# Reading a key/value cache in tiles of four heads instead of two, with half as many buffers

## The chip, the cores and the metric

The kernel runs on one core of a Trainium2 chip; the other cores are idle. The metric is the device time of one execution in microseconds (us). A profile is one execution with the trace on; its span runs from the first to the last instruction and is about 1.7 us shorter than the time of the same execution.

## The reference, cut to what matters

One decoding step for 8 sequences: layer norm, attention of one query per head over a cache of 4096 keys, 32 heads of 128, and in parallel a small MLP. Everything is bfloat16. The two caches together hold 537 MB of the 552 MB that the kernel reads, each byte once, and that is what the time is about.

```python
B, Sq, D = 8, 1, 640;  Hq, Hkv, Sk, Dh = 32, 32, 4096, 128
xn = _layernorm(x)
q = (xn @ wq).reshape(B, Sq, Hq, Dh).transpose(0, 2, 1, 3)
scores = einsum("bhqd,bhkd->bhqk", q, k_cache) * Dh ** -0.5      # k_cache: (8, 32, 4096, 128)
o = einsum("bhqk,bhkd->bhqd", softmax(scores), v_cache)          # v_cache: the same shape
out = x + o.transpose(0, 2, 1, 3).reshape(B, Sq, Hq * Dh) @ wo + mlp(layernorm(xn))
```

## The kernel before

A tile is two adjacent heads of one sequence: 2 MB of keys, or of values, contiguous in memory. It is spread over the 128 partitions so that each reads one run of 16 KB (64 keys of 256 B). Four key buffers and four value buffers of 16 KB per partition rotate.

```python
HT = 2                    # heads of a tile
NJ = SK * HT // P         # 64 keys per partition
T = NG * B                # 128 tiles
GT = 4                    # tiles of a softmax group
NK, NV, NS = 4, 4, 4      # key buffers, value buffers
KV_sb = sb("KV_sb", [P, NK + NV, NJ * P], BF)
...
def tile_src(cache, t):
    return cache[t % B, span(t // B, HT)].rearrange("h k d -> (h k) d").rearrange("(p j) d -> p j d", p=P)
def kpieces(t):
    return [(0, 64)]                                   # one transfer per tile
def vpieces(t):                                        # the last value tile in four transfers
    return [(0, 16), (16, 32), (32, 48), (48, 64)] if t == T - 1 else [(0, 64)]
```

All large loads are issued from the SyncE queue, in order. SyncE waits before each until the buffer is free: a key buffer when VectorE and TensorE have read it, a value buffer when TensorE has.

Per tile, a quarter of the scores is made on TensorE (transposes, ScalarE copies them out of PSUM, short matmuls) and three quarters on VectorE (multiply by the broadcast query, fold once, reduce). A softmax follows per group of tiles. Then TensorE multiplies probabilities with values (`PV_ps`), ScalarE copies the result out, and a few small matmuls gather it (`OT`). After a group of heads, the result is multiplied with rows of `wo` (loaded per group) and added up in PSUM.

```python
add("dve", dp,  mult, ...)        # Y  <- K * q          128 x 6144
add("dve", ..., fold, ...)        # Y2 <- halves added   128 x 3072
add("dve", ..., reduce, ...)      # S  <- sum            128 x 48
...
add("pe",  p0 + 0.15 * q, pe_pv)  # PV <- P^T V          16 matmuls of 512 columns per tile
add("act", p0 + 0.5, evacuate)    # E  <- PV
add("pe",  p0 + 0.8, pe_ex)       # OT <- gather E
```

A small scheduler sorts all operations by a position (the second argument of `add`) on their engine's in-order queue and places the semaphore waits; the steady part is then emitted as a loop.

## Time and profile before

| | before |
|---|---|
| time, median | 1305.2 us (4 runs, 1304.7 to 1305.5) |
| span of the profile | 1303.5 us |
| DMA busy | over 99% |
| rate in the steady part | 427.7 GB/s |
| VectorE, TensorE, ScalarE busy | 85%, 54%, 40% |

From the page of the profile, kernel before: span, busy times by engine, then, for 40 slices of the span, the busy tenths of the DMA engines and what they moved; the packets; the chain of waits by engine.

```profile
span 1303.5 us, 20261 instructions
PE 704.9 (54%) x7741; PEld 401.3 (31%) x7741; DVE 1109.6 (85%) x554; ACT 516.7 (40%) x1264; POOL 0.2 (0%) x4
...
DMA  9999999999999999999999999999999999999997
GB/s 375 423 428 425 427 427 428 429 426 429 425 430 427 428 429 426 429 426 429 427 428 428 427 428 427 428 426 428 427 428 427 428 427 428 427 429 429 425 428 322
DMA packets 45440, 552.03 MB, mean 424 GB/s; under 512 B 4505, under 2 KB 10993, under 8 KB 12786
...
DMA 79%; DVE 11%; PE 9%; issue 1%; ACT 0%; SPq 0%
```

Every slice but the last has the 16 DMA engines at 9 tenths or more, and the rate is flat. The chain of waits is mostly a transfer. So the kernel is bound by DMA, from 2 us to the end, and only three things can shorten it: a higher rate, a DMA queue that fills earlier, or a shorter tail.

Table of windows, kernel before (window and length in us; busy us and number of instructions for TensorE, its weight loads, VectorE, ScalarE, GpSimd; granted TensorE clock; DMA share; GB/s):

```profile
400.00:600.00 200.00, 108.62 (x1157) 60.97 (x1157) 172.96 (x81) 79.84 (x195) 0.00 (x0) 0.53 1.01 427
1290.00:1295.00 5.00, 3.72 (x40) 1.14 (x40) 0.00 (x0) 1.11 (x2) 0.00 (x0) 0.50 0.98 394
1295.00:1300.00 5.00, 3.04 (x74) 1.86 (x71) 0.17 (x1) 0.87 (x2) 0.00 (x0) 0.50 0.20 79
```

The middle is at the steady rate. In the last two windows some engines have run out of work: they do not finish together.

VectorE spends 3.34 + 1.75 + 3.35 = 8.45 us on a tile, in 9.9 us that its key and value tiles take to arrive. It is the next limit, but not the present one.

DMA issues, kernel before (count, KB, median us from issue to landing):

```profile
KV_sb<-in_A_k_cache_dram SPq DMA_DIRECT2D x128, 2048.0 KB, 33.9
KV_sb<-in_A_v_cache_dram SPq DMA_DIRECT2D x127, 2048.0 KB, 31.0
```

A transfer that takes 4.9 us at the steady rate lands 31 to 34 us after it was issued: the work of five or six others stands in the queue ahead of it.

The tail, from the timeline of the kernel before (start us, duration us, engine, line, operation, count):

```profile
1298.38 0.63 PE L609 MATMUL PV_ps<-KV_sb,P_sb 128*2 128x128 bf16 x16 [0.57 <-DMA KV_sb<-in_A_v_cache_dram]
...
1299.88 1.23 PE L644 MATMUL TR_ps<-wo_sb,oTn_sb 128*8 128x320 bf16 x4 [0.26 <-DVE oTn_sb L636]
```

After the last piece of values has landed, 16 narrow matmuls run, and then four for the output.

The trace also has one record per DMA packet, with its size and duration. 10th percentile of the durations, in ns, kernel before:

```
bytes     1280   3456   4096   7168   16384
ns          55    135    159    272     611
```

These lie on a line: 0.0368 ns per byte and 7 to 8 ns per packet.

### The profile page before, as it was taken

To read this page: it belongs to the slowest core of one execution; us is meant where nothing else is said; L and a number is where in the kernel's file an instruction comes from. 1 tells how busy PE (TensorE), PEld (TensorE's weight loads), DVE (VectorE), ACT (ScalarE), POOL (GpSimd) and SP (SyncE) were. 2 spreads that over 40 slices of the span, in tenths; PEclk is the share of its full clock that TensorE was granted. 3 is DMA by queue.
4 is the path that set the end of the run, shared out by engine and by line. 5 is a ranking of instruction groups with operands and counts; after the bars stand their busy time and mean duration, and the time that the engine had idled before them with its cause. 6 is when DMAs were issued, how large, how long until landed. Compare 5 with 4: busy or idle time off the path is not lost.

```text
span 1303.5 us, 20261 instructions
## 1 busy us (share of the span) xinstructions
PE 704.9 (54%) x7741; PEld 401.3 (31%) x7741; DVE 1109.6 (85%) x554; ACT 516.7 (40%) x1264; POOL 0.2 (0%) x4
## 2 busy tenths in 40 slices
PE   2665555555555555545555555555465555555555
PEld 2543223233223223323322232332232333223222
DVE  7989889888898888898888898888988888988881
ACT  2443344434334433433434444343344334434332
POOL 0000000000000000000000000000000000000000
PEclk9999985555555555555555555555556555555555
DMA  9999999999999999999999999999999999999997
GB/s 375 423 428 425 427 427 428 429 426 429 425 430 427 428 429 426 429 426 429 427 428 428 427 428 427 428 426 428 427 428 427 428 427 428 427 429 429 425 428 322
DMA packets 45440, 552.03 MB, mean 424 GB/s; under 512 B 4505, under 2 KB 10993, under 8 KB 12786
## 3 DMA queue, kind: packets, MB, share of 16 engines
q1 hardware_dynamic: 45392, 551.81, 99.9%
q8 instruction: 10, 0.16, 0.1%
q10 hardware_dynamic: 34, 0.02, 0.0%
q14 instruction: 4, 0.03, 0.0%
HBM read 551.80 MB, written 0.01 MB: 423 GB/s over the span
## 4 chain that ended last, share of the span: by engine, by line
DMA 79%; DVE 11%; PE 9%; issue 1%; ACT 0%; SPq 0%
DMA KV_sb<-in_A_k_cache_dram 77%; DVE Y_sb L541 9%; PE TR_ps L509 5%; PE C_ps L586 2%; PE PV_ps L612 1%; DVE S_sb L548 1%; DMA KV_sb<-in_A_v_cache_dram 1%; DMA KV_sb<-in_A_wq_dram 1%; DVE Y_sb L545 1%; ACT P_sb L575 0%; SPq L367 0%; PE TR_ps L720 0%; DVE rinv_sb L591 0%; PE TR_ps L644 0%; PE TR_ps L707 0%
## 5 line engine op out<-in xcount | busy, mean ns | idle before, releaser
L512 ACT ACTIVATE KT_sb<-TR_ps 128x1024 bf16<-128x1024 bf16 x256 | 261.3, 1023 | 637.0 <-PE TR_ps L509 636.6
L509 PE MATMUL TR_ps<-ident_bf,KV_sb 128*128 128x128 bf16 x2048 | 263.6, 311 | 416.5 <-DMA KV_sb<-in_A_k_cache_dram 416.5
L548 DVE TENSOR_REDUCE S_sb<-Y_sb 128x48 f32<-128x3072 bf16 x128 | 429.2, 3353 | 4.4
L541 DVE TENSOR_TENSOR Y_sb<-KV_sb,qbc_sb 128x6144 bf16<-128x6144 bf16 x128 | 427.6, 3340 | 4.4 <-ACT qbc_sb L482 4.4
L509 PEld LDWEIGHTS TR_ps<-ident_bf,KV_sb 128*128 128x128 bf16 x2048 | 197.5, 141 | 551.8 <-DMA KV_sb<-in_A_k_cache_dram 497.6
L612 PE MATMUL PV_ps<-KV_sb,P_sb 128*8 128x512 bf16 x2032 | 279.7, 585 | 39.1 <-DMA KV_sb<-in_A_v_cache_dram 39.0
L545 DVE TENSOR_TENSOR Y_sb<-Y_sb 128x3072 bf16<-128x3072 bf16 x128 | 224.4, 1753 | 2.3
L519 PE MATMUL S_ps<-qk_sb,KT_sb 128*128 128x2 bf16 x2048 | 90.4, 167 | 74.4 <-ACT KT_sb L512 74.4
L519 PEld LDWEIGHTS S_ps<-qk_sb,KT_sb 128*128 128x128 bf16 x2048 | 71.7, 104 | 128.6 <-ACT KT_sb L512 84.5
L591 DVE RECIPROCAL rinv_sb<-C_ps 128x8 f32<-128x8 f32 x32 | 6.6, 207 | 115.5 <-PE C_ps L586 115.5
L575 ACT ACTIVATE P_sb<-S_sb,NB_sb 64x64 bf16<-64x64 f32 x256 | 88.4, 345 | 4.2
L620 ACT ACTIVATE E_sb<-PV_ps 128x512 bf16<-128x512 f32 x128 | 75.6, 591 | 27.3 <-PE PV_ps L612 24.3
L612 PEld LDWEIGHTS PV_ps<-KV_sb,P_sb 128*8 128x8 bf16 x2032 | 39.6, 83 | 92.0 <-issue 45.6
L529 ACT ACTIVATE S_sb<-S_ps 64x16 f32<-64x16 f32 x256 | 45.5, 178 | 6.2 <-PE S_ps L519 4.7
L575 ACT ACTIVATION_READ_ACCUMULATOR P_sb<-S_sb,NB_sb 64x1 f32 x256 | 47.3, 185 | 0.0
L636 DVE TENSOR_TENSOR oTn_sb<-C_ps,rinv_sb 128x8 bf16<-128x8 f32 x32 | 5.3, 166 | 46.7 <-PE C_ps L628 36.6
L628 PE MATMUL C_ps<-sel_bf,E_sb 128*128 128x2 bf16 x508 | 33.1, 170 | 13.0 <-ACT E_sb L620 6.1
L569 ACT ACTIVATE NB_sb<-CH_ps 128x4 f32<-128x4 f32 x32 | 5.5, 173 | 76.6 <-PE CH_ps L565 76.6
L628 PEld LDWEIGHTS C_ps<-sel_bf,E_sb 128*128 128x128 bf16 x508 | 23.2, 105 | 28.1 <-ACT E_sb L620 28.1
L586 PEld LDWEIGHTS C_ps<-rs_sb,mask_f 128*128 128x128 f32 x128 | 31.2, 334 | 0.9 <-issue 0.9
L586 PE MATMUL C_ps<-rs_sb,mask_f 128*128 128x4 f32 x128 | 30.8, 346 | 0.0
L565 PE MATMUL CH_ps<-identneg,M_sb 4*64 4x4 f32 x128 | 11.5, 244 | 24.8 <-DVE M_sb L560 24.8
(81 smaller groups left out, 174.0 us busy)
## 6 DMA issues: line engine op xcount, KB each, us to landing
KV_sb<-in_A_k_cache_dram SPq DMA_DIRECT2D x128, 2048.0 KB, 33.9
KV_sb<-in_A_v_cache_dram SPq DMA_DIRECT2D x127, 2048.0 KB, 31.0
wo_sb<-in_A_wo_dram SPq DMA_DIRECT2D x16, 320.0 KB, 30.5
KV_sb<-in_A_wq_dram SPq DMA_DIRECT2D x1, 4480.0 KB, 16.0
KV_sb<-in_B_w_dram SPq DMA_DIRECT2D x1, 2160.0 KB, 20.0
KV_sb<-in_B_w_dram SPq DMA_DIRECT2D x1, 2080.0 KB, 24.8
KV_sb<-in_A_v_cache_dram SPq DMA_DIRECT2D x4, 512.0 KB, 11.8
KV_sb<-in_A_wq_dram SPq DMA_DIRECT2D x1, 640.0 KB, 9.5
```

Of the source, the lines that this page charges most:

```text
L509: r = e.transpose(TR_ps[:, it.box[0], jj * P:(jj + 1) * P], kv[:, n * BK + jj, :], ident_bf[:, :])
L512: add("act", t - 0.55 + 0.2 * n, lambda e: e.activation(KT_sb[:, m % NS, :, :].rearrange("p a b -> p (a b)"), TR_ps[:, it.box[0], :], ACT. ...
L519: r = e.matmul(S_ps[:, c:c + HT], KT_sb[:, m % NS, jj, :], qk_sb[:, :, b], start=True, stop=True)
L529: r = e.activation(S_sb[s, g % SR, i, 0:JP], S_ps[s, 0:JP * HT].rearrange("p (j a) -> p j a", a=HT)[:, :, a], ACT.Copy)
L541: return e.tensor_tensor(y, kv[:, j0:j1, :], qbc_sb[:, g % 2, i, :][:, None, :].to_broadcast([P, nj, P]), ALU.mult)
L545: lambda e, y=y, y2=y2: e.tensor_tensor(y2, y[:, :, 0:P // 2], y[:, :, P // 2:P], ALU.add),
L548: lambda e, y2=y2, j0=j0, j1=j1: e.tensor_reduce(S_sb[:, g % SR, i, j0:j1], y2, AX.X, ALU.add),
L575: r = e.activation(P_sb[s, g % PR, i, :, a, :], S_sb[s, g % SR, i, :].rearrange("p (m c) -> p m c", c=4), ACT.Exp, bias=NB_sb[s, g % 2, i: ...
L586: r = e.matmul(RS_ps[:, a * GT:(a + 1) * GT], mask_f[:, a, :], rs_sb[:, g % PR, :], start=True, stop=True)
L612: r = e.matmul(PV_ps[32 * ct:32 * ct + HT * 4, t % 2, :], P_sb[:, g % PR, i, m, :, :].rearrange("p a c -> p (a c)"), vv[:, 4 * m:4 * m + 4 ...
L620: add("act", p0 + 0.5, lambda e: e.activation(E_sb[:, t % 2, 0:ne], PV_ps[:, t % 2, 0:ne], ACT.Copy), R=[("PV", t % 2)], W=[("E", t % 2)], ...
L628: r = e.matmul(o, E_sb[:, t % 2, c * P:(c + 1) * P], sel_bf[:, c:HT * 4:4], start=(c == 0), stop=(c == 3))
```

## The change

A tile becomes four adjacent heads: 4 MB, and a run of 32 KB per partition. Since buffers are twice as large, there are two for keys and two for values. The intent is fewer and longer DMA packets at the same memory. The rest follows from it: softmax groups of two tiles, TensorE's loop over half a group of heads, work with larger tiles cut in two, the early loads reordered, the MLP's second weights in a buffer of their own, and a reworked end.

```diff
-    HT = 2
+    HT = 4
-    GT = 4
+    GT = 2
+    HB = B // 2
-    NK, NV, NS = 4, 4, 4
+    NK, NV, NS = 2, 2, 4
...
+        w2_sb = sb("w2_sb", [P, FC, D], BF)
-        Y_sb = sb("Y_sb", [P, ND, P], BF)
+        Y_sb = sb("Y_sb", [P, ND // 2, P], BF)
...
-            ld(1.9, wqb_sb, A_wq[:, QP * P:H * P]..., ["wqB"], "wqb", ["ovfree"])
+            ld(-93.0, wqb_sb, A_wq[:, QP * P:H * P]..., ["wqB"], "wqb")
 def vpieces(t):
-    return [(0, 16), (16, 32), (32, 48), (48, 64)] if t == T - 1 else [(0, 64)]
+    return [(0, 64), (64, 96), (96, NJ)] if t == T - 1 else [(0, NJ)]
...
-            pos = (-100.0, -98.0, -94.0, -93.0)[t] if t < NK else t - 3.6
+            pos = (-100.0, -94.0)[t] if t < NK else t - 1.5          # key tiles
-            pos = (1.95, 5.6, 5.65, 6.0)[t] if t < NV else pvpos(t - NV) + 0.95
-            R = (["wqAfree"] if t == 0 else ["wqBfree", "ovfree"]) if t < NV else []
+            pos = t + 0.6                                            # value tiles
+            R = (["wqBfree"], ["wqBfree", "wqAfree", "ovfree"])[t] if t < NV else []
...
-            cuts = [(JP, NJ)]
+            cuts = [(JP, JP + ND // 2), (JP + ND // 2, NJ)]
...
-            sch.emit_rolled("pe", e, sems, 6.43, B)
+            sch.emit_rolled("pe", e, sems, 2.013, HB)
```

The first value buffer still holds query weights at the start (`wqb_sb`); `wqBfree` is given when TensorE has computed the queries from them.

## The prediction

> **What bounds the kernel now.** The page: 16 DMA engines busy 99.9% of 1303.5 us, 552 MB at 424 GB/s; a table of windows: 427 to 428 GB/s from 200 to 1250 us. The chain of waits is 77% key-cache DMA. VectorE (85%), TensorE (54%) and ScalarE (40%) all have slack. The outer ends: the first packet starts 2 us in, and after the last value piece lands (PE goes on at 1298.4 us) 5 us of tail remain. [...]
>
> **What the change gives.** The trace's packet records: typical durations 55 ns (1280 B), 135 (3456), 159 (4096), 272 (7168), 611 (16384). That is a line of 0.0368 ns per byte plus 7 to 8 ns per packet. A 32 KB run as one packet should take about 1215 ns, not 1222. Each engine carries about 2040 of the 16 KB packets; 1020 times 7.3 ns saved is 7.4 us. Half as many transfers also save 127 completion packets of 9 ns per engine, 1.1 us. All of it is on the critical path: together 8.5 us. Nothing else in the steady state moves the time, as bytes are equal.
>
> **Does the DMA queue stay full with two buffers?** A pair of 4 MB tiles takes 19.6 us (twice the 9.8 us of today's pair). VectorE needs per tile 2 x (3.34 + 1.75 + 3.35) = 16.9 us plus about 0.6 for maxima and reciprocals, under 19.6. A key buffer is given back 17.5 us after landing, when two transfers, V(t-1) and K(t+2)'s slot, order the queue: K(t+2) must be issued by 29.4 us after K(t) landed. Slack about 12 us. Values have more. TensorE needs about 10 us per tile. VectorE now waits for the wo weights once in eight tiles; they land about 3 us late for it; the slack covers that.
>
> **Start and end.** Before key tile 2, 18 MB are issued without waiting, drained near 47 us. Value tile 0 overwrites the query weights, so it waits for seven projection rounds of about 1 us (measured: 0.7 us TensorE + 0.2 us ScalarE + hand-overs) after they land: about 56 us, while K2 ends at 56.5. I expect a gap of 0 to 4 us there, 1 to 2 likely. The tail grows: 32 narrow matmuls instead of 16 (0.6 to 1.0 us) and 8 output matmuls instead of 4 (1.2 to 2.4 us): +1.6 us.
>
> Sum: 1305.2 - 8.5 + 1.5 + 1.6, rounded down for the other early work, about **1299 us**, range 1291 to 1307. Chances: faster by over 2% 0.04, within 2% 0.93, slower by over 2% 0.03.
>
> **Right or wrong in the profile.** Right: packets of 32768 B near 1215 to 1225 ns; windows at 429 to 431 GB/s; DMA busy over 99%; busy times of VectorE and TensorE nearly unchanged, ScalarE a little up; SyncE's waits end long before the queue empties. Wrong: 16 KB packets still (no gain, about 1308), windows below 427 GB/s or slices with DMA under 9 tenths (buffers too few), a hole of over 5 us near 57 us.
>
> **What would break it.** [...] the engines drifting apart by whole 1.2 us packets, which lengthens the end; VectorE waiting on TensorE for maxima or reciprocals long enough to eat the 12 us of slack.

1305.2 - 8.5 + 1.5 + 1.6 = 1299.8 us, put at 1299. The 9 ns of a completion packet are in the trace of the kernel before: 4506 packets of 4 bytes, about 16 for each of the 280 loads from SyncE's queue, with a mean of 9.0 ns.

## More of the kernel before

Groups of instructions, kernel before (busy us in all, mean ns of one):

```profile
L548 DVE TENSOR_REDUCE S_sb<-Y_sb 128x48 f32<-128x3072 bf16 x128 | 429.2, 3353 | 4.4
L541 DVE TENSOR_TENSOR Y_sb<-KV_sb,qbc_sb 128x6144 bf16<-128x6144 bf16 x128 | 427.6, 3340 | 4.4 <-ACT qbc_sb L482 4.4
...
L545 DVE TENSOR_TENSOR Y_sb<-Y_sb 128x3072 bf16<-128x3072 bf16 x128 | 224.4, 1753 | 2.3
...
L620 ACT ACTIVATE E_sb<-PV_ps 128x512 bf16<-128x512 f32 x128 | 75.6, 591 | 27.3 <-PE PV_ps L612 24.3
```

## The result, and the profile after

| | before | after |
|---|---|---|
| time, median | 1305.2 us (4 runs) | 1298.78 us (4 runs, 1298.17 to 1301.47) |
| span of the profile | 1303.5 us | 1297.0 us |
| first packet to last value packet | 1296.0 us | 1288.7 us |
| last value packet to end of span | 5.6 us | 6.5 us |

The ratio is 0.9955, with a 95% interval of 0.9938 to 0.9972. Ratios here are the mean time of one kernel's fast runs over that of the other's of the same rounds, so not quite the ratio of the medians. The kernel is faster by 0.5%, which is within 2%.

The same lines of the page, kernel after:

```profile
span 1297.0 us, 19542 instructions
PE 657.6 (51%) x7884; PEld 428.4 (33%) x7884; DVE 1119.4 (86%) x574; ACT 493.1 (38%) x1202; POOL 0.2 (0%) x4
...
DMA  9999999999999999999999999999999999999997
GB/s 383 399 425 433 431 429 434 426 434 432 428 435 425 436 434 428 432 425 436 434 431 431 425 435 435 431 429 431 429 435 431 429 431 429 436 430 426 433 430 302
DMA packets 26738, 552.04 MB, mean 426 GB/s; under 512 B 2313, under 2 KB 8801, under 8 KB 10082
...
DMA 86%; PE 9%; DVE 2%; SPq 2%; issue 1%; ACT 0%; DVEq 0%
```

There are 26,738 packets instead of 45,440, and the steady slices are higher: the 64 + 64 cache tiles now move in packets of 32 KB. But the second slice is lower than it was (399 against 423 GB/s), and so is the last. The clock line of TensorE is not shown; it is at 9 tenths or more in the first slice and at 5 or 6 after it, where the kernel before had 8 or 9 tenths in its first six slices and 5 or 6 after them.

Table of windows, kernel after:

```profile
50.00:60.00 10.00, 8.04 (x175) 7.16 (x173) 4.85 (x2) 4.42 (x10) 0.00 (x0) 0.50 0.91 356
400.00:600.00 200.00, 101.02 (x1182) 65.24 (x1180) 174.94 (x84) 77.39 (x189) 0.00 (x0) 0.54 1.01 431
1280.00:1290.00 10.00, 8.52 (x76) 2.96 (x76) 0.22 (x2) 1.88 (x6) 0.00 (x0) 0.71 0.77 320
1290.00:1295.00 5.00, 3.10 (x45) 1.41 (x42) 0.47 (x2) 0.58 (x2) 0.00 (x0) 0.77 0.00 2
```

In 400 to 600 us the rate is 431 GB/s against 427. The window 50 to 60 us has a hole: 356 GB/s at a DMA share of 0.91.

Groups, kernel after (the same VectorE work and ScalarE copy):

```profile
L544 DVE TENSOR_TENSOR Y_sb<-KV_sb,qbc_sb 128x6144 bf16<-128x6144 bf16 x128 | 429.1, 3352 | 93.9 <-DMA KV_sb<-in_A_k_cache_dram 93.9
L551 DVE TENSOR_REDUCE S_sb<-Y_sb 128x48 f32<-128x3072 bf16 x128 | 429.1, 3353 | 4.4
...
L548 DVE TENSOR_TENSOR Y_sb<-Y_sb 128x3072 bf16<-128x3072 bf16 x128 | 224.9, 1757 | 4.4
...
L638 ACT ACTIVATE E_sb<-PV_ps 128x512 bf16<-128x512 f32 (+1 forms) x65 | 38.5, 592 | 319.8 <-PE PV_ps L619 317.9
```

VectorE does the same 128 rounds in the same time. ScalarE's copy out of PSUM now occurs 65 times instead of 128, because a tile of four heads fills the same 512 columns; this saves it 37 us of busy time. ScalarE has no share in the chain that ended last (ACT 0%), so it saves nothing else.

DMA issues, kernel after:

```profile
KV_sb<-in_A_k_cache_dram SPq DMA_DIRECT2D x64, 4096.0 KB, 26.8
KV_sb<-in_A_v_cache_dram SPq DMA_DIRECT2D x63, 4096.0 KB, 35.2
```

A transfer takes 9.7 us now. A key tile lands 26.8 us after its issue, so about 17 us of work stand ahead of it. Two buffers are enough.

Waits of VectorE, kernel after (total us, times, longest us):

```profile
DVE Y_sb L544 <- DMA KV_sb<-in_A_k_cache_dram: 93.9, 53, 2.3
DVE oTn_sb L661 <- issue: 22.5, 8, 3.1
```

VectorE waits a little for key tiles, which is how a DMA-bound kernel should look, and eight times for the weights of `wo`, never longer than 3.1 us. (The profile names no releaser for the latter, only "issue"; but each of the seven long waits ends 0.04 us after a load of `wo` has landed.)

The hole, from the timeline of the kernel after, SyncE's issues (key tile 2, value tile 0, key tile 3):

```profile
30.97 0.34 SPq L370 DMA_DIRECT2D KV_sb<-in_A_k_cache_dram  x1
56.29 0.34 SPq L370 DMA_DIRECT2D KV_sb<-in_A_v_cache_dram  x1
60.43 0.33 SPq L370 DMA_DIRECT2D KV_sb<-in_A_k_cache_dram  x1
```

And TensorE's query projections, the first and the last of seven rounds, same kernel:

```profile
48.85 0.69 PE L457 MATMUL C_ps<-xnT_sb,KV_sb 128*128 128x8 bf16 x20 [16.87 <-DMA KV_sb<-in_A_wq_dram]
...
55.56 0.70 PE L457 MATMUL C_ps<-xnT_sb,KV_sb 128*128 128x8 bf16 x20 [0.29 <-ACT qT_sb L462]
```

Value tile 0 goes into the buffer of the query weights. They land at 48.8 us, the last round has started at 55.6 us, and the load is issued at 56.3 us, when the DMA engines have just drained key tile 2. By the packet records, 1.1 us of all 16 engines are lost there.

The balance can be read from the bytes moved by a given time (from the packet records):

```
MB moved by      50 us    60 us    200 us   1200 us   1285 us
before           19.51    23.71     83.44    511.17    547.45
after            19.59    23.10     83.31    514.25    550.84
```

From 60 to 1285 us the kernel after gains 4.00 MB, which is 9.3 us at 431 GB/s. It starts that stretch 0.61 MB behind (1.4 us, the hole and the restart after it), and the engines end 0.5 us more apart. That leaves 7.4 us, by which the last value packet comes earlier (1290.5 instead of 1297.9 us). The tail is 0.9 us longer.

### The profile page after: what moved, and what is told of

It reads as the page before. It is cut to its first block, busy times and chain, and to the rows that moved or that the text cites. A ratio compares the mean times of both kernels' runs of the same rounds, so it can differ in the third digit from the quotient of the medians.

```text
span 1297.0 us, 19542 instructions
## 1 busy us (share of the span) xinstructions
PE 657.6 (51%) x7884; PEld 428.4 (33%) x7884; DVE 1119.4 (86%) x574; ACT 493.1 (38%) x1202; POOL 0.2 (0%) x4
## 2 busy tenths in 40 slices
DMA packets 26738, 552.04 MB, mean 426 GB/s; under 512 B 2313, under 2 KB 8801, under 8 KB 10082
## 4 chain that ended last, share of the span: by engine, by line
DMA 86%; PE 9%; DVE 2%; SPq 2%; issue 1%; ACT 0%; DVEq 0%
DMA KV_sb<-in_A_v_cache_dram 84%; PE PV_ps L619 8%; DMA KV_sb<-in_A_wq_dram 2%; SPq L370 2%; DVE Y_sb L544 1%; DVE Y_sb L548 0%; PE C_ps L457 0%; PE TR_ps L512 0%; ACT KT_sb L515 0%; PE TR_ps L669 0%; ACT qT_sb L462 0%; ACT S_sb L532 0%; PE PV_ps L629 0%; PE S_ps L522 0%; DVE out_sb L749 0%
## 5 line engine op out<-in xcount | busy, mean ns | idle before, releaser
L619 PE MATMUL PV_ps<-KV_sb,P_sb 128*16 128x512 bf16 x2040 | 224.6, 619 | 130.4 <-DMA KV_sb<-in_A_v_cache_dram 130.4
L522 PE MATMUL S_ps<-qk_sb,KT_sb 128*128 128x4 bf16 x2048 | 97.9, 170 | 147.4 <-ACT KT_sb L515 145.8
L638 ACT ACTIVATE E_sb<-PV_ps 128x512 bf16<-128x512 f32 (+1 forms) x65 | 38.5, 592 | 319.8 <-PE PV_ps L619 317.9
L522 PEld LDWEIGHTS S_ps<-qk_sb,KT_sb 128*128 128x128 bf16 x2048 | 86.1, 109 | 178.2 <-ACT KT_sb L515 178.2
L619 PEld LDWEIGHTS PV_ps<-KV_sb,P_sb 128*16 128x16 bf16 x2040 | 63.1, 124 | 242.9 <-DMA KV_sb<-in_A_v_cache_dram 136.0
L583 ACT ACTIVATE P_sb<-S_sb,NB_sb 32x128 bf16<-32x128 f32 x256 | 101.9, 398 | 3.8
L644 PE MATMUL C_ps<-sel_bf,E_sb 128*128 128x4 bf16 x256 | 16.9, 172 | 102.6 <-DVE rinv_sb L600 79.3
L532 ACT ACTIVATE S_sb<-S_ps 32x32 f32<-32x32 f32 x256 | 48.2, 188 | 31.5 <-PE S_ps L522 29.2
L583 ACT ACTIVATION_READ_ACCUMULATOR P_sb<-S_sb,NB_sb 32x1 f32 x256 | 47.0, 184 | 0.0
L595 PE MATMUL C_ps<-rs_sb,mask_f 128*128 128x2 f32 x256 | 45.4, 299 | 0.0
L661 DVE TENSOR_TENSOR oTn_sb<-C_ps,rinv_sb 128x8 bf16<-128x8 f32 x32 | 4.7, 147 | 26.8 <-issue 22.5
## 6 DMA issues: line engine op xcount, KB each, us to landing
KV_sb<-in_A_k_cache_dram SPq DMA_DIRECT2D x64, 4096.0 KB, 26.8
KV_sb<-in_A_v_cache_dram SPq DMA_DIRECT2D x1, 2048.0 KB, 12.7
```

Source lines behind the costliest of these rows:

```text
L522: r = e.matmul(S_ps[:, c:c + HT], KT_sb[:, m % NS, jj, :], qk_sb[:, :, b % HB], start=True, stop=True)
L532: r = e.activation(S_sb[s, g % SR, i, 0:JP], S_ps[s, 0:JP * HT].rearrange("p (j a) -> p j a", a=HT)[:, :, a], ACT.Copy)
L583: r = e.activation(P_sb[s, g % PR, i, :, a, :], S_sb[s, g % SR, i, :].rearrange("p (m c) -> p m c", c=4), ACT.Exp, bias=NB_sb[s, g % 2, i: ...
L595: r = e.matmul(RS_ps[:, a * GT:(a + 1) * GT], mask_f[:, a, :], rs_sb[:, g % PR, :], start=True, stop=True)
L619: r = e.matmul(PV_ps[32 * ct:32 * ct + HT * 4, t % 2, :], P_sb[:, g % PR, i, m, :, :].rearrange("p a c -> p (a c)"), vv[:, 4 * m:4 * m + 4 ...
L638: add("act", pos, lambda e: e.activation(E_sb[:, k, 0:n], PV_ps[:, k, 0:n], ACT.Copy), R=[("PV", k)], W=[("E", k)], X=[("PVb", k)])
```

## The experiments

The edited kernels start from the kernel after; where one builds on another edit, it says so. All results were correct. "Tile time" is the time per 4 MB of cache in the steady part: from the packet records, the time between the reading of one amount of cache and the same amount plus 96 tiles of 4 MB, over 96. It includes a sixteenth of a load of `wo`, and repeats to 0.002 us between the three traces of the kernel after. The expectations give the tail (last value packet to end of span) 0.25 us shorter than this document: packet times had first been read 0.25 us late against the instructions.

Theory P: the gain in the steady part is a fixed cost per DMA packet. Rivals: the other parts of the change (S), easier addresses for the memory (A), or the number of transfers (T).

### The kernel after, once more (a0_again)

> The changed kernel once more, as the reference for the others of this call and to see its spread (one of its first four times was 1301.5, the other three 1298.2 to 1298.8). Every theory: 1298 to 1302 us.

Measured: 1299.75 us (1297.81, 1300.93, 1301.30, 1298.57), ratio 0.9960 to before. The spread is in two groups, which comes up again below. Kernel before in these rounds: 1305.39 us.

### Packets of 16 KB in two transfers (e1_two_16k)

```diff
 def kpieces(t):
-    return [(0, NJ)]
+    return [(0, 64), (64, 128)]
 def vpieces(t):
-    return [(0, 64), (64, 96), (96, NJ)] if t == T - 1 else [(0, NJ)]
+    return [(0, 64), (64, 96), (96, NJ)] if t == T - 1 else [(0, 64), (64, 128)]
```

> Changed kernel, but every tile of 4 MB is loaded by two transfers, each with runs of 16 KB: the packets and the number of transfers are those of the kernel before, everything else is the change's. Theory P (the gain is a fixed cost of about 7 ns per packet and 9 ns per completion): packets of 611 to 615 ns, steady rate back to 427.7 GB/s, and 8 to 9 us lost: about 1307 us, over the kernel before, whose start has no hole. Rival S (the gain comes from the other parts, the order of the early loads, the smaller tail, the half quads): time stays at 1299.

Measured: 1310.52 us (1309.16 to 1311.56), 10.8 us over the kernel after. Kernels are compared only within the same rounds. Window of the steady part, this run:

```profile
400.00:600.00 200.00, 102.36 (x1174) 65.12 (x1173) 173.64 (x84) 75.94 (x185) 0.00 (x0) 0.51 1.01 427
```

The rate is that of the kernel before, and the tile time is 9.903 us: before it was 9.903 us too, and after it is 9.828 us. So the whole gain in the steady part hangs on the size of the packets or on the number of transfers, and rival S is out: the other parts of the change are all present here, and the time is worse than before. That it is 3.5 us over the expected 1307 is partly the larger cost per packet and partly this run's tail, of 8.7 us.

### Packets of 16 KB in one transfer (e5_one_16k)

```diff
-        KV_sb = sb("KV_sb", [P, NK + NV, NJ * P], BF)
+        PAD = 32                                  # 64 bytes between the halves of a buffer
+        HJ = NJ // 2
+        HW = HJ * P + PAD
+        KV_sb = sb("KV_sb", [P, NK + NV, 2 * HW], BF)
...
+                return s.rearrange("p (h j) d -> p h (j d)", h=2)   # the source: 128 x 2 x 8192
...
-            cuts = [(JP, JP + ND // 2), (JP + ND // 2, NJ)]
+            cuts = [(JP, HJ), (HJ, HJ + 32), (HJ + 32, NJ)]
```

> Changed kernel, one transfer per 4 MB tile as there, reading the same addresses in the same order per partition, but 64 bytes of padding between the halves of each buffer so that a run written is 16 KB; VectorE takes three cuts of 32 columns instead of two of 48 for that. Theory P: packets of 16 KB at 611 to 615 ns, 7.4 us lost, about 1306 us (1 us less than with two transfers). Rival A (longer runs are easier on the memory, whatever the packet): the addresses read are unchanged, so about 1299. If the queue makes 32 KB packets in spite of the padding, it says nothing.

Measured: 1307.36 us (1305.25 to 1309.58, in two groups), packets of 16 KB, tile time 9.879 us. Window of the steady part, this run:

```profile
400.00:600.00 200.00, 102.34 (x1188) 66.73 (x1185) 177.68 (x115) 76.69 (x188) 0.00 (x0) 0.54 1.01 428
```

The addresses read are those of the kernel after, in the same order per partition, and 0.051 of the 0.075 us per tile are lost all the same. So most of the gain is not in the addresses (rival A): shorter packets alone cost it. The remaining 0.025 us per tile between this run and the last would fit a cost per transfer, but see the run with every second partition.

### Packets of 8 KB (e2_four_8k)

```diff
 def kpieces(t):
-    return [(0, NJ)]
+    return [(0, 32), (32, 64), (64, 96), (96, 128)]
```

and the same for the value tiles but the last.

> Changed kernel, every tile by four transfers with runs of 8 KB. From the time per 4 MB tile in three traces (9.828 us with 32 KB, 9.879 with 16 KB in one transfer, 9.903 with 16 KB in two) come 6.4 ns per packet and 24.5 ns per transfer; with 16 packets per engine and two transfers more that makes 10.055 us per tile, and 127.5 tiles x 0.152 us = 19 us more than the run with two transfers of 16 KB: about 1328 us. Packet records of 309 to 315 ns. If the law is wrong and small runs cost more than their packets (or the memory minds), the time is well above 1332; if only the packet's own 7.3 ns count, 1325.

Measured: 1327.46 us (two runs), ratio 1.0168; tile time 10.055 us. Window of the steady part, this run:

```profile
400.00:600.00 200.00, 102.39 (x1145) 59.62 (x1144) 170.35 (x82) 74.92 (x185) 0.00 (x0) 0.51 1.01 421
```

The time came out as expected, but it does not test the split in the expectation, since packets and transfers grow together here. The tile times are on a straight line in the number of packets per engine, 8, 16 and 32:

```
                       packets per engine and 4 MB      tile time, us       difference per packet
after                         8                             9.828
two transfers of 16 KB       16                             9.903              0.0757 / 8  = 9.5 ns
four transfers of 8 KB       32                            10.055              0.1513 / 16 = 9.5 ns
```

So a packet costs 9.5 ns beside its bytes, where each 8 packets come with a transfer of their own.

### Twice the transfers, packets of 32 KB: halves of the partitions (e3_half_parts)

```diff
-                ld(pos + 0.01 * n, kview(t)[:, j0:j1, :], lambda ...: tile_src(A_k_cache, t)[:, j0:j1, :], ...)
+                for u in range(2):
+                    s = slice(64 * u, 64 * u + 64)
+                    ld(pos + 0.01 * n + 0.005 * u, kview(t)[s, j0:j1, :],
+                       lambda ...: tile_src(A_k_cache, t)[s, j0:j1, :], ...)
```

and the same for values; readers wait for both halves.

> Changed kernel, every tile loaded by two transfers of 64 partitions each, runs of 32 KB: the number of transfers of before, the packets of after. Theory P: only the 9 ns completions come back, 1.1 us: about 1300 us. Rival T (it is the number of transfers that costs, not the packets): about 1306 or more. [...]

Measured: 2602.69 us, ratio 1.9932. Window of the steady part, this run:

```profile
400.00:600.00 200.00, 48.89 (x598) 32.34 (x598) 86.48 (x40) 36.45 (x87) 0.00 (x0) 0.55 1.01 211
```

Neither theory expected this. All engines are busy (DMA share 1.01), yet the rate is half, and a packet of 32 KB takes 2391 to 2564 ns instead of 1213 to 1221 (10th and 90th percentile). The 211 GB/s are close to half of 430.9, the steady rate of the kernel after; why the rate halves, this run does not show.

### Twice the transfers, packets of 32 KB: every second partition (e8_alternate)

```diff
-                    s = slice(64 * u, 64 * u + 64)
+                    s = slice(u, P, 2)
```

(from the kernel with halves)

> The run with half partitions again, but a transfer now takes every second partition instead of one half of the partitions: again 64 partitions and runs of 32 KB per transfer, twice the transfers. Theory H (what halved the rate there was that all 16 engines write into one half of the partitions at once): rate back to 430 GB/s, packets near 1215 to 1225 ns, and the cost of twice the transfers alone, which the runs with 16 KB put at 24 ns each, so 3 us: about 1302 us. Rival N (64 partitions per transfer are slow whatever they are, or two transfers per tile are): 2600 us again.

Measured: 1299.22 us (1298.85 to 1301.55), ratio 0.9951; tile time 9.828 us. Window of the steady part, this run:

```profile
400.00:600.00 200.00, 102.75 (x1186) 67.44 (x1183) 175.07 (x85) 77.03 (x187) 0.00 (x0) 0.54 1.00 430
```

The full rate is back with 64 partitions per transfer and two transfers per tile, so it was which partitions, not how many. By what means they halve the rate, no trace shows. It also decides rival T: twice as many transfers, with the packets unchanged, cost nothing that the tile time shows. The expected 24 ns per transfer fell. The gain is in the packets. What the 0.025 us between one and two transfers of 16 KB is, stays open. The records say only that the packets of the run with one transfer were 1 ns shorter on the mean (613.9 instead of 614.9 ns), 0.017 us in the 16 packets of a tile.

### The hole at the start (e4_wqb_first), beside the kernel after (a1_again)

```diff
-            ld(-93.0, wqb_sb, A_wq[:, QP * P:H * P]..., ["wqB"], "wqb")
+            ld(-94.5, wqb_sb, A_wq[:, QP * P:H * P]..., ["wqB"], "wqb")
```

This issues the big load of query weights before key tile 1.

> The changed kernel again, as the reference of this call. In eight times so far it fell in two groups, five of 1297.8 to 1298.8 and three of 1300.9 to 1301.5. My reading of the traces so far: the groups are the granted TensorE clock in the last 10 us (1.00 or 0.50), where TensorE's own work is the longest chain; expected again two groups 3 us apart, and in the profile a tail (last value packet to end of span) of 5.3 us at clock 1.00, 6 to 8.4 us at 0.50.

Measured: 1299.58 us (1300.04, 1300.30, 1299.58, 1298.67, 1298.17). The two groups were not clear this time. The profiled one had a tail of 7.5 us. Its TensorE clock was 0.50 until 1.6 us after the last value packet, and 1.00 from there on.

> Changed kernel, with the big load of query weights issued before key tile 1 instead of after it, so that value tile 0 (which overwrites them) is released 10 us earlier. If the hole in the DMA queue near 57 us (1.1 us of all engines in two traces) is due to that wait: no idle engine between 50 and 60 us, last value packet about 1.1 us earlier, times 1 us lower in both groups. If the queue would have run dry anyway (VectorE gets key tile 1 later): the hole moves or grows.

Measured: 1296.91 us (1300.04, 1296.02, 1299.02, 1296.91, 1296.03), ratio 0.9934. Window of the hole, this run:

```profile
50.00:60.00 10.00, 6.97 (x146) 6.01 (x143) 9.93 (x4) 5.43 (x11) 0.00 (x0) 1.00 0.99 418
```

The rate there is 418 GB/s instead of 356, the idle time between 50 and 60 us is 0.1 us instead of 1.1 to 1.8, and the last value packet comes at 1288.8 us instead of 1290.4 to 1290.7. So the wait for the query weights was the hole, and it cost 1.5 to 2 us. The best times fell by that much (1298.2 to 1296.0); but the profiled execution took 1300.0 us, as if nothing had been gained.

### The two groups (e6_tail, e7_both, e9_base_early, e10_warm)

That execution shows where the gain went. Its tail and its clock, from the timeline and the table of windows of the run with early query weights:

```profile
1287.96 2.74 PE L619 MATMUL PV_ps<-KV_sb,P_sb 128*16 128x512 bf16 x24
...
1291.61 1.06 PE L629 MATMUL PV_ps<-KV_sb,P_sb 128*4 128x128 bf16 x32
...
1293.53 2.30 PE L669 MATMUL TR_ps<-wo_sb,oTn_sb 128*8 128x320 bf16 x8 [0.26 <-DVE oTn_sb L661]
```

```profile
1289.00:1298.00 9.00, 5.44 (x61) 2.22 (x53) 0.65 (x2) 1.30 (x3) 0.00 (x0) 0.50 0.01 1
```

The last value packet came at 1288.8 us, but the narrow matmuls that use it start only at 1291.6: TensorE is still busy with earlier value tiles, at half its clock (0.50). The same work in the repeat of the kernel after, whose tail ran at clock 1.00 (its last value packet came at 1290.4 us):

```profile
1290.83 0.65 PE L629 MATMUL PV_ps<-KV_sb,P_sb 128*4 128x128 bf16 x32 [0.22 <-DMA KV_sb<-in_A_v_cache_dram]
...
1292.35 1.25 PE L669 MATMUL TR_ps<-wo_sb,oTn_sb 128*8 128x320 bf16 x8 [0.26 <-DVE oTn_sb L661]
```

```profile
1290.60:1295.90 5.30, 2.10 (x42) 1.18 (x41) 0.65 (x2) 0.70 (x2) 0.00 (x0) 1.00 0.01 2
```

Narrow matmuls 0.65 us instead of 1.06, output matmuls 1.25 instead of 2.30, and no lateness. Only 0.50 and 1.00 occur in these tails. In the clock records of the kernels before and after, which have no other value either, each stretch between two changes lasts 3.41 us or a whole multiple of it. What decided between the two in an execution, no run shows.

Theory C: in the last 10 us TensorE is the longest chain, and its granted clock makes the groups. The first edit took work out of that chain:

```diff
-        fp = T - 0.5                                       # the base sum: copy, transposes, add, float32 matmuls
+        fp = T - 1.05
-        add("pe", fp + .02, pe_fin, ...)
+        add("pe", fp + .01, pe_fin, ...)
-        add("dve", fp + .04, dve_base, ...)
+        add("dve", fp + .10, dve_base, ...)
-        add("pe", fp + .06, pe_base, ...)
+        add("pe", fp + .25, pe_base, ...)
-            rp = ... else pvpos(T - 1) - 0.04              # the last row sums
+            rp = ... else pvpos(T - 2) - 0.04
```

> Changed kernel, with the base sum (transposes, residual, 2.3 us of float32 matmuls) and the last row sums taken out of TensorE's queue ahead of the last two value tiles, to places where it waits for DMA. Theory C (the 3 us between the groups is TensorE's work at half clock on the last chain): the upper group moves down by 2 us or more, the lower stays within 0.5 us; all times within 1297 to 1299.5. Rival (the groups come from the DMA engines, which end at different times): both groups stay.

Measured: 1300.63 us (1297.04, 1300.86, 1299.49, 1300.92, 1300.63), ratio 0.9961. This is a miss: the slow group stayed. The profile, of the fast execution (clock 1.00 in the tail), shows a fault of the edit: with the row sums ahead of it, the second last value tile waits for the last exponentials, so that TensorE starts that tile at 1283.6 us, no earlier than in the kernel after (1282.3 to 1283.3 us in three traces). There is no trace of one of its slow executions. By the expectation, this result spoke for the rival (DMA engines that end at different times). The three traces of the kernel after speak against it: their last value packets lie within 0.4 us (1290.4 to 1290.7 us), their spans 2.3 us apart (1296.0 to 1298.3 us).

> Both edits, early query weights and shorter tail: if they are as reasoned, 1296 to 1298.5 us in all times, the best of all kernels here, 0.7% under the kernel before.

Measured: 1296.14 us (1296.14, 1296.12, 1297.15, 1296.06, 1296.23), ratio 0.9930 with an interval of 0.9916 to 0.9943. This is the best kernel. Its profile has clock 1.00 from 1285 us to the end and a tail of 5.6 us. But the same tail edit alone was slow four times in five, so the steadiness of these five times is not explained by the edits, and its cause is not shown.

The next kernel has the early query weights and the base sum of the first edit, but the row sums in their old place, and gathers the wide part of the last tile after the narrow matmuls:

```diff
-            rp = ... else pvpos(T - 2) - 0.04
+            rp = ... else pvpos(T - 1) - 0.04
-            add("pe", p0 + (0.14 if last else 0.28), pe_ex, ...)
+            add("pe", p0 + (0.265 if last else 0.28), pe_ex, ...)
```

> Early query weights, the base sum moved out of the last chain, but the row sums back in their old place (before, they made the second last value tile wait for the last exponentials, which I had overlooked in the tail edit), and the wide part of the last tile gathered after the narrow matmuls instead of ahead of them. Theory C (TensorE's granted clock in the last 10 us makes the groups): the slow group comes closer, 1296 to 1298 in all times; a profile at clock 0.50 in the tail shows narrow matmuls at most 1.5 us after the last value packet (2.6 us with early query weights alone).

Measured: 1297.50 us (1297.28 to 1297.66, five runs in one group), ratio 0.9938. The profiled execution had clock 0.50 through the whole tail. Timeline and window, this run:

```profile
1289.22 1.06 PE L629 MATMUL PV_ps<-KV_sb,P_sb 128*4 128x128 bf16 x32 [1.00 <-DMA KV_sb<-in_A_v_cache_dram]
...
1291.14 2.30 PE L669 MATMUL TR_ps<-wo_sb,oTn_sb 128*8 128x320 bf16 x8 [0.26 <-DVE oTn_sb L661]
```

```profile
1289.00:1295.80 6.80, 3.74 (x45) 1.92 (x45) 0.65 (x2) 0.70 (x2) 0.00 (x0) 0.50 0.01 2
```

The last value packet came at 1288.7 us, as in the run with early query weights alone (1288.8), and the clock was the same 0.50. Now TensorE waits for the packet and starts 0.5 us after it, where it had started 2.8 us after it. The tail is 7.1 us instead of 9.4 us. This is the clean comparison of two executions: same data, same clock, work taken out of the chain. It narrowed the spread of the times from 4.0 to 0.4 us. It did not measurably lower their mean: the ratio is 0.9938, against 0.9934 with early query weights alone (in another call), whose best time was 1.3 us lower.

The last kernel adds six unused matmuls in TensorE's wait for the second last value tile, to have the clock raised:

```diff
+        def pe_warm(e):
+            for _ in range(6):
+                r = e.matmul(S_ps[:, :], ident_bf[:, :], KT_sb[:, 0, 0:4, :].rearrange("p a b -> p (a b)"), start=True, stop=True)
+            return r
+        add("pe", T - 0.1, pe_warm, R=["ident", ("KT", 0)], W=["warm"], X=["S"])
```

> The same with six idle 512-column matmuls (result unused) in TensorE's wait for the second last value tile, to have the clock raised before the last chain. Theory C: clock 1.00 from about 1285 us on in the profile and all five times in one group, 1295.5 to 1296.5. If the groups stay, the clock is not what makes them.

Measured: 1297.31 us (1296.96 to 1297.77), ratio 0.9938: one group, but not the expected 1295.5 to 1296.5. The clock rose at 1282.8 us (in the kernel after, without these matmuls, at 1285.9 us, so that they raised it is not shown) and fell back to 0.50 at 1289.6 us, soon after 1.9 us of waiting for the last packet, and the output matmuls took 2.30 us again. The warming cost nothing and gained nothing that the times show.

Tails of the profiles, from the last value packet to the end of the span:

| kernel | tail, us | narrow matmuls start after the packet, us | clock in it |
|---|---|---|---|
| before | 5.6 | (ahead of it, in pieces) | 0.50 |
| after | 6.5 | 0.5 | 1.00, then 0.50 from 1292.7 us |
| after, repeats | 5.6; 7.5 | 0.5; 2.4 | 1.00; 0.50, then 1.00 from 1292.3 us |
| two transfers of 16 KB | 8.7 | 2.1 | 0.50 |
| one transfer, 16 KB | 6.3 | 1.2 | 1.00 |
| four transfers of 8 KB | 7.1 | 0.5 | 0.50 |
| halves of the partitions | 7.1 | 0.5 | 0.50 |
| every second partition | 9.4 | 2.8 | 0.50 |
| early query weights | 9.4 | 2.8 | 0.50 |
| tail edit; both edits | 5.7; 5.6 | 0.6; 0.5 | 1.00 |
| base sum early | 7.1 | 0.5 | 0.50 |
| with warming | 6.7 | 0.5 | 1.00, then 0.50 from 1289.6 us |

From the start of the narrow matmuls to the end of the span, the edited kernels and the kernel after take 5.1 us in all five traces where the clock is then 1.00, 6.6 us in all six where it is 0.50, and 6.0 and 6.2 us in the two where it falls in between. The rest of the tail is how late these matmuls start.

The kernel before had clock 0.50 and still 5.6 us: with half the work per value tile (16 wide matmuls instead of 32), TensorE is not late there even at that clock, and nine times differ by 0.8 us only. That the clock and this chain make the spread of the kernel after is shown for the profiled executions; for those without a trace it is inferred.

## Why the prediction was right, point by point

- **Time.** Predicted 1299 us, range 1291 to 1307; measured 1298.78 us. Within 2%, as given 0.93.
- **What bounds it.** Right: DMA. The steady rate rose from 427.7 to 430.9 GB/s. The slices of 436 in the page count a packet whole where it begins; with packets spread over their durations, no 5 us of the steady part of the kernel after pass 433.3 GB/s. A limit of the rate is not shown.
- **Packets.** Right in kind: 32 KB packets at 1213 to 1221 ns (predicted 1215 to 1225). The size of the term was a little small. I took 7.3 ns per packet and 9 ns per completion, 8.5 us together. The tile times give 0.075 us per tile, 9.5 ns per packet, and 127 x 0.075 = 9.5 us. So the term that was mis-sized is the cost per packet. My line went through the fastest tenths of packets up to 16 KB; between 16 and 32 KB these give 2 x 611 - 1213 = 9 ns, and the mean durations (615.1 and 1217.5 ns from 200 to 1200 us) give 12.7 ns. The records alone give the cost to a few ns only. The separate cost per completion was not seen: twice the transfers cost nothing.
- **Two buffers suffice.** Right: no idle DMA engine between 60 and 1280 us. I worked out 12 us of slack; a key load had about 17 us of work ahead of it. The wait for `wo`, put at about 3 us, was 3.0 to 3.1 us.
- **The hole.** Right in place, cause and size: expected 0 to 4 us near 57 us, measured 1.1 to 1.8 us idle in three traces. Undoing the cause gained 1.5 to 2 us.
- **The tail.** Predicted +1.6 us; +0.9 us in the profile. I costed the matmuls at the clock of the trace of before, 0.50, and took it for given. At that clock, and with TensorE on time, the costing holds: with packets of 8 KB and the same end the tail is 7.1 us, +1.5. But the tail of the kernel after took 5.6, 6.5 and 7.5 us in three traces, by the granted clock and by how late TensorE was, and 9.4 us with every second partition and the same end.
- **The sum.** Predicted -8.5 + 1.5 + 1.6 = -5.4 us, then rounded down to 1299. In the profile: -9.3 (packets) + 1.4 (hole) + 0.5 (engines ending apart) + 0.9 (tail) = -6.5 us. That the median lies within 0.3 us of 1299 is partly luck: the rounding covered the 1 us that the sum lacked, and the tail alone varies by 1.9 us between three traces.
- **ScalarE "a little up".** Wrong: 516.7 to 493.1 us. I counted more exponential work (88.4 to 101.9 us) but not that copies out of PSUM halve (75.6 to 38.5 us). It is off the critical path.
- **Engines ending apart, named as a risk.** 0.5 us more, as the balance above shows.

## What to carry to other kernels

When all DMA engines are busy, fit the durations of packets of different sizes in the trace you already have: the intercept, times the packets that a change removes, estimates the gain. Here it gave 7.4 us (8.5 with the completions), and the tile times 9.5 us; from runs of 16 to 32 KB that was 0.76% of the tile time (9.903 to 9.828 us). Keep transfers on all 128 partitions, or at least spread them over all: a contiguous half of the partitions per transfer halved the rate here (211 GB/s), every second partition per transfer did not (430 GB/s). After such a gain, look at the last 10 us again, because work per last tile grows with the tile, and an engine with an uncertain clock may become the end of the chain: here TensorE ran at 0.50 or 1.00, and the tail of one kernel took from 5.6 to 7.5 us in three profiles.
